# Moving one product per head pair to GpSimd and its mask to ScalarE, with reordered VectorE steps

## The chip, the cores and the metric

The kernel runs on one core of a Trainium2 chip. The metric is the device time of one execution in microseconds (us): 1022.77 us before the change, the median of three runs from 1022.21 to 1023.84. All profile times are of one profiled execution whose span is 1027.5 us.

The engines are named as the profile names them: PE is TensorE (matmuls and transposes), DVE is VectorE, ACT is ScalarE, POOL is GpSimd, SP issues the DMAs.

## The reference

For 8 batches and 8 heads, with 576 rows of 64 numbers each:

```
scores = (q @ k.T) / sqrt(64)                 # 576 x 576 per head
kth    = the 32nd largest score of each row
scores = where(scores >= kth, scores, -1e9)
attn   = softmax(scores);  out = attn @ v
```

The heads of a row are then joined to 512 numbers, and 4608 such rows go through a mixture of experts: a gate picks one of 8 experts per row, each expert keeps the 80 rows with the largest gate weight, and for these two matmuls with a relu between them are computed. All other rows of the output are zero. This change touches the attention part alone.

## The kernel before

**Pairs and units.** Two heads are handled together as a pair; there are 32 pairs. The 576 query rows of a pair are cut into four blocks of 128 rows and one of 64. A unit is one head's block (128 rows by 576 scores). The 64-row blocks of both heads lie in one unit, since together they fill 128 partitions. So a pair has 9 units: places 0 to 7 are head 0 and head 1 of block 0, 1, 2, 3, and place 8 is the joint last unit. There are 288 units in all (NU). "Odd" units are those whose work is shifted away from DVE; before the change these are places 1, 3, 5 and 7.

**What a unit needs.** `front` computes scores on PE into a PSUM tile of four banks, of which there is only one (`four`, tag `sp`), and ACT copies them to the SBUF tile `s` (L206). DVE finds the 24 largest scores of each row: six maxima of 96 columns (`parts`, L213), then three maxima and two replacements over these 48 candidates (`search`, L224 and L232). ACT then writes `sign`, the sign of (24th largest minus score), and counts it (L229). The product `y` = s times sign (L236) makes another maximum over the whole row (L238, `w<-y`) give the largest scores below the 24th. The small operation `pick` (L241) selects the threshold by the count. The `mask` of scores below the threshold is made by POOL for even units (L254, a compare) and by ACT for odd ones (L250, a relu). `turn_w` transposes the scores on PE (L286) and adds the mask by further matmuls on top (L291); ACT takes the exponentials (L293, L295) into `wT`; `back` multiplies by v on PE (L309); `divide` scales the result on ACT (L330).

**The pipeline.** The order of all instructions is written out by hand in `run`. Each call of `step(i)` starts one unit and carries older ones on: unit i has its six maxima taken, unit i-1 its search, unit i-2 its product, unit i-3 its large maximum, unit i-4 its pick and mask. A string of letters gives the order of the DVE work in a step: G is one maximum of 96 columns; a, b, c, d, e are the five stages of the search (after e, ACT's sign is issued); y is the product; g the maximum over y; h the pick; m the mask; z the reciprocals (L321). After the letters, the step issues `turn_w` for unit i-4 when a block is complete, `divide`, `front` for unit i+4, `back` for unit i-5, the transposes of the next pair's q and k (`turn`), and one piece of `norm`, which for a finished pair transposes the output (copied by L342), multiplies it by the gate weights (L347) and copies these few columns out on ACT (L353, `part`). Each engine executes its instructions in exactly this order. A step below is named by its place: the step of place p handles the maxima of place p and the mask of place p-4 (counted round the pair).

So in the step of place 3, the order is: mask of place 8; sign of place 2; then on PE `turn_w` of place 8 (transposes, then the mask matmuls), `back` of place 7, and L347; on ACT the exponentials of place 8 and the copy of `part`. In the step of place 4 follow, on PE, `front` and `back` of place 8, and in the step of place 5 `turn_w` of places 0 and 1.

**Which engine the product runs on.** For odd units POOL, for the others DVE:

```
engine = nc.gpsimd if i in self.odd else nc.vector
engine.tensor_tensor(out=y, in0=s, in1=sign, op=Alu.mult)
```

There is one `y` buffer, two of `sign`, three of `mask` and two of `wT`. POOL gets, in program order, the mask of unit i-4 ahead of the product of unit i-2.

## Time and profile before

| engine | busy us | share of the span | instructions |
|---|---|---|---|
| PE (matmul) | 902.3 | 88% | 13381 |
| DVE | 896.0 | 87% | 5087 |
| ACT | 786.2 | 77% | 1671 |
| POOL | 456.1 | 44% | 331 |

The attention part takes the first 890 us or so; the rest is routing and the experts. The busy share alone does not say who sets the pace, because an instruction that is held up after it has started counts as busy. The groups of instructions concerned:

| line, engine, what | count | mean ns |
|---|---|---|
| L236 DVE product | 160 | 739 |
| L236 POOL product | 128 | 1281 |
| L254 POOL mask | 159 | 1721 |
| L250 ACT mask | 128 | 777 |
| L241 DVE pick | 288 | 290 |
| L189 ACT copies of qT, kT | 32 + 32 | 642, 647 |

### The profile page before, as it was taken

Reading aid. Unit: us, or ns where it says so; the run is one execution under the profiler, and the core shown is the slowest. Engines: PE = TensorE matmul, PEld = TensorE weight load, DVE = VectorE, ACT = ScalarE, POOL = GpSimd, SP = SyncE. Lnnn points to the kernel's source line nnn. Section 1 sums busy time; section 2 is a strip of 40 time slices with the busy share of each in tenths; the row PEclk is TensorE's granted clock in tenths of the full one; section 3 lists DMA queues with packets and bytes.
Section 4 is the critical chain, followed back from the end, with each engine's and each line's share of the span. In section 5 each row is a group of like instructions: output and inputs, shape, how many; then the busy total and the mean of one; then the engine's idle time right before and its main releaser. Section 6 shows DMA issues by size and latency. Waiting matters only on the chain.

```text
span 1027.5 us, 35579 instructions
## 1 busy us (share of the span) xinstructions
PE 902.3 (88%) x13381; PEld 728.9 (71%) x13381; DVE 896.0 (87%) x5087; ACT 786.2 (77%) x1671; POOL 456.1 (44%) x331
## 2 busy tenths in 40 slices
PE   5889999999889999989899999998999998598896
PEld 3677777777667777777677777776777777588886
DVE  3999999999999999999999999999999999551000
ACT  3888899888888898888898888898888988401110
POOL 1444555554454545554454544555454554211101
PEclk9999999999999999999999999999999999879998
DMA  4344443333333323233333311111221200326800
GB/s 93 77 118 129 122 128 89 89 89 89 90 88 89 80 72 81 77 81 84 85 89 89 89 41 38 46 45 48 48 49 48 49 13 14 119 77 214 325 23 25
DMA packets 167893, 85.76 MB, mean 83 GB/s; under 512 B 117792, under 2 KB 154656, under 8 KB 167712
## 3 DMA queue, kind: packets, MB, share of 16 engines
q1 hardware_dynamic: 166688, 80.78, 28.4%
q0 software_dynamic: 1024, 2.62, 0.8%
q8 instruction: 107, 1.75, 0.7%
q14 instruction: 74, 0.61, 0.2%
HBM read 63.19 MB, written 20.19 MB: 81 GB/s over the span
## 4 chain that ended last, share of the span: by engine, by line
DVE 54%; PE 30%; ACT 11%; issue 2%; another core or an unknown queue 1%; DMA 0%; SPq 0%; POOL 0%; POOLq 0%; ACTq 0%; DVEq 0%
DVE cand L213 17%; DVE w L238 12%; PE cc L309 7%; DVE cand L232 6%; DVE y L236 6%; DVE pick L241 4%; DVE top L224 4%; PE yp L776 3%; PE sp L201 3%; PE ab L286 3%; ACT wT L295 3%; PE sp L178 2%; ACT sign L229 2%; PE warm L632 2%; DVE w L224 2%
## 5 line engine op out<-in xcount | busy, mean ns | idle before, releaser
L213 DVE MAX8 cand<-s 128x8 f32<-128x96 f32 x1728 | 387.0, 244 | 9.5 <-ACT s L206 9.5
L254 POOL TENSOR_SCALAR mask<-s,thr_all 128x576 bf16<-128x576 f32 x159 | 273.7, 1721 | 199.6 <-PE ab L291 130.6
L309 PEld LDWEIGHTS cc<-vb,wT 128*64 128x64 f32 x5760 | 201.2, 139 | 111.5 <-ACT wT L295 94.6
L236 POOL TENSOR_TENSOR y<-s,sign 128x576 f32<-128x576 f32 x128 | 164.0, 1281 | 240.3 <-ACT sign L229 104.2
L309 PE MATMUL cc<-vb,wT 128*64 128x65 f32 x5760 | 223.4, 225 | 52.1 <-ACT wT L295 52.1
L229 ACT ACTIVATE sign<-s,w 128x576 bf16<-128x576 f32 x288 | 226.0, 785 | 44.9 <-DVE w L224 44.5
L238 DVE MAX8 w<-y 128x8 f32<-128x576 f32 x288 | 217.4, 755 | 2.2 <-POOL y L236 2.0
L201 PE MATMUL sp<-kT,qT 64*128 64x288 f32 (+1 forms) x1280 | 202.0, 435 | 14.7 <-ACT part L353 6.1
L286 PE MATMUL ab<-ident,s 128*128 128x128 f32 x1152 | 176.5, 282 | 10.9 <-ACT wT L295 10.9
L206 ACT ACTIVATE s<-sp 128x1152 f32<-128x1152 f32 (+1 forms) x160 | 167.2, 1045 | 11.4 <-PE sp L201 9.8
L286 PEld LDWEIGHTS ab<-ident,s 128*128 128x128 f32 x1152 | 128.3, 142 | 34.6 <-ACT wT L295 25.1
L295 ACT ACTIVATE wT<-ab 128x1024 f32<-128x1024 f32 (+1 forms) x160 | 150.8, 942 | 0.0
L201 PEld LDWEIGHTS sp<-kT,qT 64*128 64x128 f32 (+1 forms) x1280 | 105.5, 179 | 53.4 <-ACT part L353 8.0
L236 DVE TENSOR_TENSOR y<-s,sign 128x576 f32<-128x576 f32 x160 | 118.2, 739 | 3.1 <-ACT sign L229 2.6
L224 DVE MAX8 top<-cand 128x8 f32<-128x48 f32 x576 | 114.4, 199 | 0.1
L291 PEld LDWEIGHTS <-mask 128*128 128x128 bf16 x1440 | 94.5, 98 | 25.8 <-ACT mask L250 19.0
L232 DVE MATCH_REPLACE8 cand<-top,cand 128x48 f32<-128x48 f32 x576 | 110.0, 191 | 0.0
L250 ACT ACTIVATE mask<-s,thr_all 128x576 bf16<-128x576 f32 x128 | 99.5, 777 | 0.4 <-DVE pick L241 0.4
L330 ACT ACTIVATE xn<-cc,z_all 128x64 f32<-128x64 f32 (+1 forms) x320 | 82.8, 316 | 2.3 <-DVE z_all L321 2.3
L241 DVE SCALAR_TENSOR_TENSOR pick<-past,cnt,w 128x9 f32<-128x9 f32 x288 | 83.6, 290 | 0.0
L286 PE MATMUL cc<-ident,s 128*128 128x128 f32 x288 | 79.0, 274 | 0.2 <-ACT xn L330 0.2
L293 ACT ACTIVATE wT<-cc 128x256 f32<-128x256 f32 (+1 forms) x160 | 57.5, 359 | 6.0 <-PE cc L291 4.4
(192 smaller groups left out, 981.5 us busy)
## 6 DMA issues: line engine op xcount, KB each, us to landing
w<-in_moe_w_dram SPq DMA_DIRECT2D x32, 512.0 KB, 4.3
w<-in_moe_w_dram SPq DMA_DIRECT2D x8, 2048.0 KB, 12.6
out_dram<-zero SPq DMA_DIRECT2D x9, 1024.0 KB, 5.9
qn<-in_q_dram SPq DMA_DIRECT2D x64, 128.0 KB, 2.4
kn<-in_k_dram SPq DMA_DIRECT2D x64, 128.0 KB, 2.5
vb<-in_v_dram SPq DMA_DIRECT2D x64, 128.0 KB, 2.5
xd<-xn SPq DMA_DIRECT2D x32, 256.0 KB, 4.1
qn<-in_q_dram SPq DMA_DIRECT2D x32, 32.0 KB, 2.3
```

The lines of the kernel that those rows point to most:

```text
L201: nc.tensor.matmul(o, lhsT=qT[d, t * P : t * P + m], rhs=kT[d, j * HS : (j + 1) * HS], start=True, stop=True)
L206: nc.scalar.activation(s[:, : g * S].rearrange("p (j c) -> p j c", c=HS), ps[:, : 2 * g, :HS], Act.Copy, scale=TINY)
L213: nc.vector.max(out=cand[:, j, :], in_=s[:, j * S // NG : (j + 1) * S // NG])
L224: nc.vector.max(out=dst, in_=cand)
L229: nc.scalar.activation(sign, s, Act.Sign, bias=w9[:, 7:8], scale=-1.0, accum_out=cnt)
L232: nc.vector.match_replace(out=cand, in_to_replace=dst, in_values=cand, imm_value=LOW)
L236: engine.tensor_tensor(out=y, in0=s, in1=sign, op=Alu.mult)
L238: nc.vector.max(out=w9[:, 8:], in_=y)
L254: engine.tensor_scalar(self.mask[i], self.s[i], self.thr[:, i : i + 1], None, op0=Alu.is_lt)
L286: nc.tensor.matmul(dst[h][c], lhsT=sc[:, keys[c]], rhs=ident, start=c == 0 or (c == NF and h == 0), stop=False, is_transpose=True, skip_gr ...
L295: nc.scalar.activation(wT[:, : g * NF, :], ab.rearrange("p h c r -> p (h c) r")[:, : g * NF, :], Act.Exp, scale=scale / TINY)
L309: nc.tensor.matmul(cc[r : r + TL, o], lhsT=wT[:, j * NF + c if c < NF else 2 * NF + j, r0 : r0 + TL], rhs=vb[:, c, h, :], start=(c == 0), ...
```

## The change

Place 8 of each pair becomes odd too. Its product moves from DVE to POOL, and its mask from POOL (DVE for the very last unit) to ACT, where the matmul with `huge` replaces that with `minus`. The order of the letters is rewritten: where unit i-3 is odd, so that its product was made by POOL in the step before, two maxima and one replacement (G, b, G) are put ahead of the pick; otherwise the large maximum g goes first and the pick after it. The sign (after e) comes early where unit i-1 is odd. The copies of the transposed q and k out of PSUM become one operation.

```
-            self.turned[n] = [self.qkp.tile([P, S], F32, name=name, tag=name) for name in ("qT", "kT")]
-            for j in range(2):
-                nc.scalar.copy(self.turned[n][j], ps[j][:, :S])
+            both = self.qkp.tile([P, 2, S], F32, name="both", tag="both")
+            nc.scalar.copy(both, four.rearrange("p (k j) c -> p k (j c)", k=2)[:, :, :S])
+            self.turned[n] = both[:, 0, :], both[:, 1, :]
...
-            engine = nc.vector if i == NU - 1 else nc.gpsimd
-            engine.tensor_scalar(self.mask[i], self.s[i], self.thr[:, i : i + 1], None, op0=Alu.is_lt)
+            nc.gpsimd.tensor_scalar(self.mask[i], self.s[i], self.thr[:, i : i + 1], None, op0=Alu.is_lt)
...
-            self.odd = {i for i, unit in enumerate(units) if unit[2] == 1}
+            self.odd = {i for i, unit in enumerate(units) if unit[2] > 0}
...
-                for c in "hmgyGbGcGdGGGeaz" if i - 2 in self.odd else "hmgGbGcGdGeGGyaz":
+                head = "GbGhmg" if i - 3 in self.odd else "ghmGbG"
+                rest = "GeGGa" if i - 1 in self.odd else "GGGea"
+                for c in head + ("ycGd" + rest if i - 2 in self.odd else "cGd" + rest[:-1] + "ya") + "z":
```

What it is for: DVE has one product less per pair, and the pick, a DVE operation with two tensor inputs, comes later in the steps that follow a POOL product.

## The prediction

> **What bounds the kernel now.** I read the windows first, then the groups, then the timelines of four engines over one pair. In the window from 300 to 400 us (columns: window, its length, busy PE, weight loads, DVE, ACT, POOL, then granted clock, DMA share and GB/s):

> ```profile
> 300.00:400.00 100.00, 90.69 (x1277) 72.32 (x1277) 100.00 (x583) 89.77 (x190) 50.26 (x34) 1.00 0.34 90
> ```

> DVE is busy 100.00 of 100 us, so it sets the pace. But PE and ACT stand at 90%, and each waits for the other inside; whether they have room must be seen in their order. A group of instructions (count, busy us and mean ns, idle time before them), and one line of the waits (total us, times, longest):

> ```profile
> L236 DVE TENSOR_TENSOR y<-s,sign 128x576 f32<-128x576 f32 x160 | 118.2, 739 | 3.1 <-ACT sign L229 2.6
> ```

> ```profile
> ACT sign L229 <- DVE w L224: 44.5, 67, 1.5
> ```

> ACT waits for DVE only 44.5 us in 32 pairs, 1.4 us per pair, two waits of about 0.6. Now the timelines. POOL and DVE at the end of one pair's heavy part:

> ```profile
> 345.19 1.72 POOL L254 TENSOR_SCALAR mask<-s,thr_all 128x576 bf16<-128x576 f32 x1 [4.61 <-PE ab L291]
> 346.88 1.28 POOL L236 TENSOR_TENSOR y<-s,sign 128x576 f32<-128x576 f32 x1
> ```

> ```profile
> 347.25 0.93 DVE L241 SCALAR_TENSOR_TENSOR pick<-past,cnt,w 128x9 f32<-128x9 f32 x1
> ```

> A pick normally takes 0.21; this one ends at 348.18, just as POOL's product ends at 348.16. It was held by that product, 0.8 us in every pair, and is counted as busy. ACT, then PE, in the steps of places 2 to 5:

> ```profile
> 347.72 1.16 ACT L206 ACTIVATE s<-sp 128x1152 f32<-128x1152 f32 x1
> 348.73 0.81 ACT L229 ACTIVATE sign<-s,w 128x576 bf16<-128x576 f32 x1
> ...
> 350.45 0.19 ACT L353 COPY part<-sp 128x40 f32<-128x40 f32 x1 [0.16 <-PE sp L347]
> ...
> 353.87 0.78 ACT L229 ACTIVATE sign<-s,w 128x576 bf16<-128x576 f32 x1 [0.63 <-DVE w L224]
> 354.55 0.19 ACT L229 ACTIVATION_READ_ACCUMULATOR sign<-s,w 128x1 f32 x1
> 354.80 0.38 ACT L293 ACTIVATE wT<-cc 128x256 f32<-128x256 f32 x1
> ```

> ```profile
> 348.11 0.22 PE L291 MATMUL cc<-minus,mask 128*128 128x128 bf16 x1
> 348.16 0.39 PE L291 MATMUL ab<-minus,mask 128*128 128x128 bf16 x4
> 348.48 1.39 PE L309 MATMUL cc<-vb,wT 128*64 128x65 f32 x40
> 349.69 0.71 PE L347 MATMUL sp<-wg,xT 128*64 128x8 f32 x20
> 350.69 1.19 PE L201 MATMUL sp<-kT,qT 64*64 64x288 f32 x8 [0.29 <-ACT part L353]
> 351.81 1.38 PE L309 MATMUL cc<-vb,wT 128*64 128x65 f32 x20
> 353.12 0.66 PE L286 MATMUL ab<-ident,s 128*128 128x128 f32 x4
> ...
> 354.55 0.22 PE L291 MATMUL cc<-huge,mask 128*128 128x128 bf16 x1
> ```

> PE runs without a gap, but for `part`, from place 8's mask matmuls (348.11) to those of places 0 and 1, after which ACT's exponential can start (354.80). The sign at 348.73 comes about 1.5 us after its input was ready: ACT is behind here, which costs nothing as long as POOL made the mask in time.

> [...] a DVE product ran from 878.91 to 879.67 in its usual 0.76 us while a mask ran from 877.95 to 879.67, so a mask holds nothing after its first 0.96 us. [...]

> **Part by part.** A step of DVE from start to start in the timeline: pick 0.13, g 0.67, six G 0.98, b and d 0.17 each, c, e 0.11 each, a 0.12: 2.46 us; 3.12 with a product (0.66). Nine steps before: 9 x 2.46 + 5 x 0.66 + reciprocals and the gate addition 0.45 + the held pick 0.80 = 26.7; the trace has 26.73 from one pair to the next.

> *Product of place 8 to POOL.* Takes 0.66 off DVE per pair. But in the step of place 1 POOL now has the mask of place 6 and then the product of place 8. Before, the same double stood in the step of place 3 (mask of 8, product of 1). From a pick the chain is 0.39 + 1.72 + 1.28 = 3.37 us, and the next pick comes 2.47 later, in the old order and in the new (both picks move by the same G, b, G, 0.5 us). So the hold of 0.8 stays, moved from the step of place 4 to that of place 2. POOL's sum falls (32 products of 1.28 for 31 masks of 1.72).

> *Later picks.* They keep picks clear of late products in the steps of places 4, 6, 8: worth the 0.1 seen at place 8 in some pairs. Pick to DVE product shrinks from 2.34 to 1.84 us, while POOL's mask ends 2.11 after the pick. If masks excluded products to their end, three products per pair would lose 0.27 each; I take zero, by the 878.91 line, and keep 0.8 for the range. DVE alone would then need 26.73 - 0.66 = 26.07 per pair.

> *One copy for two.* Starts of the two are 0.54 + 0.53 apart; one of 1152 columns takes 1.01 like the score copy (347.72 to 348.73). Saves 0.06 of ACT.

> *Mask of place 8 to ACT.* It goes in ahead of the sign at 348.73 and adds 0.68 (start of a mask to start of a following sign). ACT gets there at 348.73 - 0.06 = 348.67, whatever DVE does, for ACT has no wait on DVE from the sign at 332.78 on. Queued behind it: on ACT the sign of place 2; on PE, which now waits for it, everything from 348.11 on. A mask takes 0.79 and PE starts 0.05 later, so at 349.51 instead of 348.11. Then mask matmuls 0.37, `back` 1.21, L347 up to the copy 0.76: `part` at 351.85 instead of 350.45, **1.40 later**.

> That closes a loop of ACT and PE. Before: exponential 328.08 to the sign of place 6, without its wait 4.03; that sign (332.78) to the sign of place 2 (348.73) 15.95, all ACT or PE work that ACT waits for (the q and k transposes 1 us among it); to `part` 1.72; to the next such exponential 4.35. Sum 26.05: 0.68 shorter than DVE's 26.73, which is why it isn't seen. After: 26.05 + 1.40 = **27.45**. The old slack takes 0.68 of the 1.40 and 0.72 per pair is lost. DVE, with 26.07 of work, will then stand waiting.

> *Sum.* 31 rounds x 0.72 = 22.3. Three rounds before are longer on DVE by the gate work, 1.85 each (27.84 + 27.47 against 2 x 26.73); about half of that will hide in DVE's idle time: -2.8. At the end, mask and product of the last unit on slower engines: DVE's mask was 0.52, ACT's is 0.78 behind exponentials, +0.7. Together +20.2: **1043 us**.

> **The rivals.** *Faster, DVE's law:* ACT and PE follow after all and each pair gains 0.66: 32 x 0.66 - 0.7 = 20.4, so 1002. For it speaks the 100% of DVE; against it the 1.40 above, over twice the slack. *No change:* the mask costs ACT 0.62 but PE does not pass the delay on to `part`; then the product of place 2 still waits for its sign. Its slack is 0.75 now (350.40 against 349.64), and DVE comes 0.66 earlier, ACT 0.62 later, so it loses 0.55 or so and 0.1 per pair is left: 1021. *Masks exclude products:* DVE at 26.07 + 0.81 = 26.88, 31 x 0.15 = 5: 1028, if the loop is not there. *The loop at full weight:* nothing of the 1.40 absorbed, 31 x 1.40 = 43: 1066. *The hold goes away as well:* 32 x 1.46: 976; it needs POOL's 3.37 to fit in 2.47.

> **How the numbers follow.** Forecast 0.65, DVE's law 0.15, no change 0.12, masks exclude 0.03, full weight 0.03, hold gone 0.02. The range leaves out DVE's law, the hold and the full weight (0.20): from 1018, below the no-change case, to 1050, if gate work hides nothing and a lowered PE clock lengthens the loop. Slower: 0.65 + 0.03 + 0.03 and 0.03 of the no-change case = 0.74; same 0.05; faster 0.21.

> **What would show it.** PE's wait ahead of L291 for ACT's mask grows from 12.7 us to over 40; ACT waits ahead of `part` about 1 us per pair (4.5 us in all before) and ahead of the exponential of place 1 about 0.8; ACT's wait for DVE's `w` nearly vanishes; DVE is no longer at 100%, with waits before L236 for ACT's sign; pairs are 27.4 us apart. A held pick of about 0.9 us stands in the step of place 2. It would be wrong if ACT reached place 8's mask early, or if PE made up the 1.4 us before `part`.

## The result and the profile after

The changed kernel takes 1069.68 us (median, 1063.06 to 1073.34) against 1022.49 us for the kernel before: a ratio of 1.0455, with a 95% interval from 1.0392 to 1.0517. It is slower, as forecast, but by 47 us where 20 were forecast, and it lies outside the range that ended at 1050. Its runs are spread over 10 us; those of the kernel before over 3.

The windows of the kernel after (window, its length, then busy PE, weight loads, DVE, ACT, POOL, granted clock, DMA share, GB/s), and the row of the page with the granted PE clock in 40 slices:

```profile
100.00:200.00 100.00, 88.17 (x1160) 68.93 (x1159) 90.88 (x526) 83.42 (x176) 44.27 (x31) 0.93 0.37 96
300.00:400.00 100.00, 87.16 (x1228) 68.58 (x1226) 95.74 (x553) 88.07 (x183) 47.02 (x32) 1.00 0.29 75
```

```profile
PEclk9999989889899999998899999989999999988999
```

In the window from 300 to 400 us DVE has fallen from 100.00 to 95.74: it no longer sets the pace. In the window from 100 to 200 there is something else: the clock is 0.93 and DVE is busy only 90.88. Slices with an 8 in the clock's row are scattered over the whole attention part.

Pairs are therefore of two kinds. Measured from one pair to the next at the same operation of DVE (the last maximum of the search, L224, for place 6), the period is 27.62 us where the clock is full, 26.73 before; and about 2.9 us more in 8 of 31 pairs. The waits of the kernel after (us in total, times, longest), and the first of them in the kernel before:

```profile
PE cc L289 <- ACT mask L250: 53.1, 65, 1.3
DVE z_all L319 <- PE cc L307: 30.7, 39, 4.8
ACT part L351 <- PE sp L345: 29.2, 23, 2.3
ACT wT L291 <- PE cc L289: 28.9, 32, 2.0
DVE lg L354 <- ACT part L351: 17.6, 22, 2.6
ACT sign L229 <- DVE w L224: 8.6, 15, 0.8
```

```profile
PE cc L291 <- ACT mask L250: 12.7, 30, 0.4
```

(Lines after L188 have moved: the mask matmuls are L289, `back` is L307, the gate weights' matmul L345, `part` L351, the exponentials L291 and L293.) PE's wait for ACT's mask has gone from 12.7 to 53.1 us, ACT waits for PE twice per pair, and ACT's wait for DVE has shrunk from 44.5 to 8.6. One pair at full clock, PE first, around place 8's mask matmuls:

```profile
650.99 0.66 PE L284 MATMUL ab<-ident,s 128*128 128x128 f32 x4 [0.32 <-ACT wT L293]
653.09 0.23 PE L289 MATMUL cc<-huge,mask 128*128 128x128 bf16 x1 [1.33 <-ACT mask L250]
...
653.47 1.39 PE L307 MATMUL cc<-vb,wT 128*64 128x65 f32 x40
655.68 1.19 PE L201 MATMUL sp<-both 64*64 64x288 f32 x8 [0.29 <-ACT lg L351]
```

Then ACT in the same steps:

```profile
652.23 0.80 ACT L250 ACTIVATE mask<-s,thr_all 128x576 bf16<-128x576 f32 x1
652.89 0.80 ACT L229 ACTIVATE sign<-s,w 128x576 bf16<-128x576 f32 x1
...
655.44 0.19 ACT L351 COPY lg<-sp 128x40 f32<-128x40 f32 x1 [1.00 <-PE sp L345]
...
659.79 0.38 ACT L291 ACTIVATE wT<-cc 128x256 f32<-128x256 f32 x1 [0.75 <-PE cc L289]
...
664.02 0.78 ACT L229 ACTIVATE sign<-s,w 128x576 bf16<-128x576 f32 x1
```

And DVE:

```profile
653.82 0.76 DVE L236 TENSOR_TENSOR y<-s,sign 128x576 f32<-128x576 f32 x1 [0.30 <-ACT sign L229]
654.90 0.17 DVE L319 RECIPROCAL z_all<-cc 128x2 f32<-128x2 f32 x1 [0.21 <-PE cc L307]
658.29 0.16 DVE L319 RECIPROCAL z_all<-cc 64x2 f32<-64x2 f32 x1 [0.74 <-ACT mask L250]
663.72 0.20 DVE L224 MAX8 w<-cand 128x8 f32<-128x48 f32 x1
672.80 0.92 DVE L241 SCALAR_TENSOR_TENSOR pick<-past,cnt,w 128x9 f32<-128x9 f32 x1
```

The loop of the forecast stands here: PE waits 1.33 us for the mask that ACT reaches at 652.23, the copy of the gate result follows late, ACT waits for it (1.00) and again for PE at the exponential (0.75). The held pick (672.80, 0.92) now stands in the step of place 2. DVE waits too: for the sign, and twice for the reciprocals of `back`'s sums. The 0.74 ahead of the second is put down to ACT's mask, but that had ended at its usual time; the reciprocal reads what `back` of place 8 writes, a matmul group that started at 656.80 and took 1.38, and it starts as that ends.

The slow pairs look different. Here is PE at the same place in one of them:

```profile
134.90 0.23 PE L289 MATMUL cc<-huge,mask 128*128 128x128 bf16 x1 [1.33 <-ACT mask L250]
...
135.28 2.09 PE L307 MATMUL cc<-vb,wT 128*64 128x65 f32 x40
137.15 1.19 PE L345 MATMUL sp<-wg,xT 128*64 128x8 f32 x20
138.63 2.19 PE L201 MATMUL sp<-both 64*64 64x288 f32 x8 [0.28 <-ACT part L351]
140.74 2.20 PE L307 MATMUL cc<-vb,wT 128*64 128x65 f32 x20
```

The wait is the same 1.33 us, but right after it `back` takes 2.09 us instead of 1.39, the scores of place 8 take 2.19 instead of 1.19, and the next `back` 2.20 instead of 1.38. The trace also records each change of the granted clock. In this execution it has only two values, 1 and 0.5, and all its changes lie on one grid of 3.41 us. These are windows of that grid, four around this wait and two around the wait (up to 341.7) of a pair at full clock:

```profile
132.31:135.73 3.42, 1.78 (x26) 1.28 (x26) 3.14 (x21) 3.42 (x9) 2.33 (x2) 1.00 0.09 19
135.73:139.14 3.41, 3.12 (x55) 2.81 (x52) 1.48 (x5) 1.28 (x4) 0.00 (x0) 0.50 0.03 7
139.14:142.55 3.41, 3.41 (x25) 2.28 (x22) 2.15 (x16) 2.24 (x7) 1.27 (x1) 0.50 0.00 0
142.55:145.97 3.42, 3.42 (x36) 2.69 (x35) 2.99 (x17) 1.84 (x6) 1.72 (x1) 1.00 0.58 148
...
337.12:340.53 3.41, 2.54 (x21) 1.52 (x18) 3.41 (x24) 3.41 (x8) 1.28 (x1) 1.00 0.50 112
340.53:343.95 3.42, 2.28 (x65) 2.11 (x65) 2.90 (x15) 2.49 (x6) 1.72 (x1) 1.00 0.02 5
```

The clock is half for two windows, 6.83 us, and it falls at the end of a window in which PE was busy 1.78 us. In the other pair the same weak stretch of PE is split between two windows, with 2.54 and 2.28 us busy, and the clock stays full. The place on the grid separates all pairs: in the 8 slow ones the wait ends 2.57 to 2.75 us into a window, in the 23 others 0.63 to 2.44 us into one. (Busy time as the profile shows it does not separate them: five windows with 1.77 or 1.78 us busy, whose waits end at 2.40 to 2.44, brought no drop.) Slow pairs without gate work take 30.54 us: 30.54 - 27.62 = 2.9 us for a stretch.

So the profiled run (1072.98 us, near the top of the spread) divides like this, measured from place 6 of the first pair to place 6 of the last: 883.3 us against 835.6, 47.7 more; the 8 slow pairs, about 2.9 us each, are 23.4 of them, the clock's part, and 24.3 are the longer loop.

### The profile page after: what moved, and what is told of

It reads as the page before. It is cut to its first block, busy times and chain, and to the rows that moved or that the text cites. A ratio compares the mean times of both kernels' runs of the same rounds, so it can differ in the third digit from the quotient of the medians.

```text
span 1070.8 us, 35577 instructions
## 1 busy us (share of the span) xinstructions
PE 924.3 (86%) x13381; PEld 740.3 (69%) x13381; DVE 886.4 (83%) x5054; ACT 800.7 (75%) x1671; POOL 443.6 (41%) x332
## 4 chain that ended last, share of the span: by engine, by line
PE 38%; ACT 32%; DVE 25%; issue 4%; POOL 0%; DMA 0%; SPq 0%; ACTq 0%; POOLq 0%; DVEq 0%
PE cc L307 13%; DVE cand L213 8%; ACT wT L293 7%; ACT sign L229 6%; ACT s L206 6%; ACT mask L250 6%; DVE w L238 5%; PE sp L201 5%; PE sp L178 4%; PE yp L776 4%; DVE cand L232 3%; DVE y L236 3%; ACT wT L291 2%; PE ab L284 2%; ACT xn L328 2%
## 5 line engine op out<-in xcount | busy, mean ns | idle before, releaser
L213 DVE MAX8 cand<-s 128x8 f32<-128x96 f32 x1728 | 392.4, 248 | 10.1 <-ACT s L206 9.5
L236 POOL TENSOR_TENSOR y<-s,sign 128x576 f32<-128x576 f32 x160 | 205.0, 1281 | 361.4 <-ACT sign L229 128.5
L307 PEld LDWEIGHTS cc<-vb,wT 128*64 128x64 f32 x5760 | 211.0, 143 | 98.7 <-ACT wT L293 78.4
L252 POOL TENSOR_SCALAR mask<-s,thr_all 128x576 bf16<-128x576 f32 x128 | 220.3, 1721 | 139.6 <-DVE pick L241 130.8
L307 PE MATMUL cc<-vb,wT 128*64 128x65 f32 x5760 | 233.5, 230 | 35.8 <-ACT wT L293 35.8
L229 ACT ACTIVATE sign<-s,w 128x576 bf16<-128x576 f32 x288 | 225.0, 781 | 11.2 <-DVE w L224 8.6
L201 PE MATMUL sp<-both 64*128 64x288 f32 (+1 forms) x1280 | 210.0, 449 | 14.5 <-ACT part L351 6.1
L206 ACT ACTIVATE s<-sp 128x1152 f32<-128x1152 f32 (+1 forms) x160 | 167.0, 1044 | 23.0 <-PE sp L201 23.0
L293 ACT ACTIVATE wT<-ab 128x1024 f32<-128x1024 f32 (+1 forms) x160 | 150.2, 939 | 0.0
L201 PEld LDWEIGHTS sp<-both 64*128 64x128 f32 (+1 forms) x1280 | 107.8, 183 | 55.4 <-ACT part L351 8.0
L289 PEld LDWEIGHTS <-mask 128*128 128x128 bf16 x1440 | 91.5, 98 | 71.3 <-ACT mask L250 65.7
L250 ACT ACTIVATE mask<-s,thr_all 128x576 bf16<-128x576 f32 x160 | 124.9, 780 | 1.2 <-DVE pick L241 1.0
L224 DVE MAX8 top<-cand 128x8 f32<-128x48 f32 x576 | 115.9, 201 | 1.1
L236 DVE TENSOR_TENSOR y<-s,sign 128x576 f32<-128x576 f32 x128 | 95.5, 746 | 10.2 <-ACT sign L229 10.0
L241 DVE SCALAR_TENSOR_TENSOR pick<-past,cnt,w 128x9 f32<-128x9 f32 x288 | 83.5, 290 | 0.0
L289 PE MATMUL cc<-huge,mask 128*128 128x128 bf16 x160 | 36.4, 227 | 53.1 <-ACT mask L250 53.1
```

The lines of the kernel that those rows point to most:

```text
L201: nc.tensor.matmul(o, lhsT=qT[d, t * P : t * P + m], rhs=kT[d, j * HS : (j + 1) * HS], start=True, stop=True)
L206: nc.scalar.activation(s[:, : g * S].rearrange("p (j c) -> p j c", c=HS), ps[:, : 2 * g, :HS], Act.Copy, scale=TINY)
L213: nc.vector.max(out=cand[:, j, :], in_=s[:, j * S // NG : (j + 1) * S // NG])
L229: nc.scalar.activation(sign, s, Act.Sign, bias=w9[:, 7:8], scale=-1.0, accum_out=cnt)
L250: nc.scalar.activation(self.mask[i], self.s[i], Act.Relu, bias=self.thr[:, i : i + 1], scale=-1.0)
L252: nc.gpsimd.tensor_scalar(self.mask[i], self.s[i], self.thr[:, i : i + 1], None, op0=Alu.is_lt)
```

## The experiments

The theory after the result was: the loop of ACT and PE is as long as forecast and gives half of the loss; the idle 1.3 us on PE brings half-clock stretches, which give the other half. The rivals: the mask on ACT costs in another way (ACT's own time, or a branch through DVE); the product or the new order are to blame; the slow clock has nothing to do with the idle stretch. All ratios are to the kernel before, run on the same chip.

**The mask of place 8 alone on ACT** (kernel before, product on DVE, old order; the mask matmul takes `huge` with it; `self.last` holds the units of place 8):

```
-            if i in self.odd:
+            if i in self.odd or i in self.last:
                 nc.scalar.activation(self.mask[i], ...)
```

> The kernel before with one edit: the mask of place 8 goes to ACT (product of place 8 stays on DVE, old order of the letters, two copies). Theory (the mask, late in ACT's queue, holds PE up and closes the loop of ACT and PE, and the gap on PE lets its clock drop): pairs 27.6 us apart where the clock is full, stretches at half clock as in the changed kernel, 1050 to 1075 us. Rival (the product on POOL or the new order of the letters costs the time; DVE alone sets the pace): the pick of the step of place 4 is no longer held, since POOL has no mask ahead of the product of place 1, so 26.73 - 0.80 per pair and about 998 us.

Measured: 1090.51 us, 1.0600 (1.0544 to 1.0657). The mask alone brings the loss, and a larger one than the whole change; the time also lies above the 1075 expected at most. A pair at full clock takes 28.2 us (27.62 in the whole change), and 5 pairs have half-clock stretches, again just those whose wait ends in one part of the grid (2.55 to 2.88 us into a window). The trace shows waits that go with the extra 0.6; DVE, then ACT of this kernel:

```profile
606.27 0.20 DVE L356 TENSOR_TENSOR lg<-lg,part 128x40 f32<-128x40 f32 x1 [0.59 <-ACT part L353]
```

```profile
592.52 0.78 ACT L229 ACTIVATE sign<-s,w 128x576 bf16<-128x576 f32 x1 [0.45 <-DVE w L224]
```

In the pairs that have a gate addition, three of four, the late `part` holds up this addition on DVE, DVE is then late with `w`, and ACT's sign waits for it. In the others, DVE waits 0.74 us for the sums of a late `back` instead. A branch of the loop runs through DVE; the forecast had none.

**The product of place 8 alone on POOL** (kernel before, mask on POOL, old order; the letter y stands where that order has it for POOL's products):

```
-            engine = nc.gpsimd if i in self.odd else nc.vector
+            engine = nc.gpsimd if i in self.odd or i in self.last else nc.vector
```

> The kernel before with one edit: the product of place 8 goes to POOL (mask of place 8 stays on POOL, old order, two copies). Theory: no effect on the loop of ACT and PE; DVE loses 0.66 of work per pair and gains a second held pick of about 0.8 in the step of place 2, so 26.9 per pair and 1022 to 1030 us, clock as before. Rival (the product on POOL is what costs): 1045 us or more.

Measured: 1032.32 us, 1.0037 (1.0022 to 1.0051); 26.88 us per pair. DVE's 0.66 is taken off, but POOL now runs late in two steps and two picks per pair are held (0.92 and 0.91) where it was one: + 0.70. That makes 26.77; the last 0.1 was not traced. The forecast's argument that a mask followed by a product on POOL makes a held pick stands, here twice.

**PE kept busy while it waits** (kernel after, 12 matmuls on zeros into a part of `ab` that this unit does not use, between the transposes and the mask matmuls of place 8):

```
+            if g == 1:
+                for _ in range(12):
+                    nc.tensor.matmul(<256 columns of ab, bank 1>, lhsT=zeros, rhs=zeros, start=True, stop=True)
             for h in range(g):
                 mk = self.mask.pop(i + h)
```

> The changed kernel with twelve idle matmuls of 256 columns on PE between the transposes and the mask matmuls of place 8, whose result is never read: they fill the 1.3 us in which PE waits for ACT's mask. Theory (the gap makes the PE clock drop, and the drops are what the forecast of 1043 lacked): mean clock 0.985 or more, pairs 27.6 apart throughout, 1040 to 1047 us. Rival (the clock drops for another reason, such as the amount of PE work, or the loss lies elsewhere): clock 0.965 to 0.975 still and 1063 to 1075 us.

Measured: 1054.99 us, 1.0277 (1.0250 to 1.0304), with a clock of 0.991 over the run (after: 0.965). PE of this kernel:

```profile
661.69 1.47 PE L289 MATMUL ab<-zero 128*128 128x256 bf16 x12
663.18 0.23 PE L293 MATMUL cc<-huge,mask 128*128 128x128 bf16 x1
```

More work on PE made the kernel faster (the time lies above the 1040 to 1047 expected, but the kernel before took 1028.36 on this chip). Apart from the first and the last few, every pair without gate work takes 27.62 us: the loop is untouched, and no half-clock stretch is left in the attention part of its trace. That shows the cause of the second half of the loss. Up to place 6 of the last pair it takes 24.1 us more than the kernel before, which is the loop, and 23.4 less than the change as it is.

**`back` of place 7 ahead of `turn_w` of place 8** (kernel after; PE has 1.2 us of work to do before it needs the mask):

```
+                joint = whole(i - 4) and units[i - 4][2] == 2
+                if joint:
+                    self.back(*units[i - 5][:2])
                 if whole(i - 4):
                     self.turn_w(*units[i - 4][:2])
```

> The changed kernel with one edit in the order of PE: in the step of place 3, back of place 7 is issued ahead of turn_w of place 8, so that PE multiplies by v while ACT makes the mask. Theory (PE's wait for the mask delays everything behind it up to the exponential of place 1): part comes about 1.2 us earlier, the loop falls to 26.4, no gap on PE in this step; pairs 26.4 apart, 1003 to 1015 us, clock 0.98 or more. Rival (ACT itself is full with one mask more, whatever PE does): 27.4 per pair and 1040 us or more.

Measured: 1024.82 us, 0.9966 (0.9953 to 0.9978); 26.63 us per pair, clock 0.984. Two calls changed places and the whole loss is gone (a ratio of 0.9966 after 1.0455): PE's order was what turned the late mask into a longer loop. The 26.4 expected was not reached, and a wait on DVE fits that (26 such waits, 10.6 us in all):

```profile
615.82 0.76 DVE L236 TENSOR_TENSOR y<-s,sign 128x576 f32<-128x576 f32 x1 [0.31 <-ACT sign L229]
```

This is the forecast's rival "no change", worked out there as 0.1 per pair won: the product of place 2 waits for its sign, which stands behind the mask in ACT's queue. Measured 26.73 - 26.63 = 0.1. That this wait alone sets the pace was not isolated.

**The mask still later** (kernel after, mask of place 8 issued behind the sign of place 2 on ACT):

```
+                if i - 4 in self.last:
+                    head, rest = "ghGbG", "GGGema"
```

> The changed kernel with the mask of place 8 moved further back in ACT's queue, behind the sign of place 2 instead of ahead of it (m after e in the step of place 3). No work is added. Theory: PE waits for the mask 0.75 us longer than 1.33, all behind it moves by that, pairs 28.2 to 28.4 apart where the clock is full, more half-clock stretches, 1085 to 1110 us. Rival (ACT's amount of work sets the pace, not the place of the mask): no change, 1063 to 1075.

Measured: 1133.45 us, 1.1074 (1.1056 to 1.1093), with a clock of 0.925. PE, then a line of the waits, then the row of the clock:

```profile
329.22 0.23 PE L289 MATMUL cc<-huge,mask 128*128 128x128 bf16 x1 [2.08 <-ACT mask L250]
```

```profile
PE cc L289 <- ACT mask L250: 76.6, 65, 2.3
```

```profile
PEclk9999898988998899989898898989998989988999
```

The wait of PE is 0.75 longer, as meant, and the loop grows by as much. Only three pairs have no half-clock stretch. They follow gate work and take 28.95 to 28.96 us; pairs at the same places take 28.20 in the change. So a plain pair at full clock would take 27.62 + 0.76 = 28.4, as expected. All 28 others have a stretch: 12 of 3.41 us, with periods of about 29.9 in plain pairs, and 16 of 6.83 us, with about 31.3. The time is above the 1110 expected at most because the longer wait brings the clock down in 28 of 31 pairs, where 1.33 us did in 8.

**The new order alone** (kernel before with the new letters, product and mask where they were):

```
-                for c in "hmgyGbGcGdGGGeaz" if i - 2 in self.odd else "hmgGbGcGdGeGGyaz":
+                head = "GbGhmg" if i - 3 in self.odd else "ghmGbG"
+                rest = "GeGGa" if i - 1 in self.odd else "GGGea"
+                for c in head + ("ycGd" + rest if i - 2 in self.odd else "cGd" + rest[:-1] + "ya") + "z":
```

> The kernel before with the new order of the letters alone (odd units, masks and copies as before). Theory: DVE still sets the pace, with the same work and about the same held pick in the step of place 4 (0.8 to 1.0 us): 26.7 to 26.95 per pair, 1020 to 1028 us. Rival (later picks delay masks and so PE): 1035 us or more.

Measured: 1027.96 us, 1.0049 (1.0032 to 1.0066); 26.95 per pair. Alone it wins nothing: the held pick takes 1.09 instead of 0.93 and stays in the step of place 4, because pick and POOL's product move together.

**The mask of place 8 on DVE** (kernel after; product on POOL, order new; the mask matmul takes `minus` with it):

```
+            engine = nc.vector if i in self.last else nc.gpsimd
+            engine.tensor_scalar(self.mask[i], self.s[i], self.thr[:, i : i + 1], None, op0=Alu.is_lt)
```

> The changed kernel with the mask of place 8 made by DVE, right after the pick, instead of ACT. The loop of ACT and PE then has its old length of 26.0; DVE has 25.3 of work, a mask of about 0.55 with its wait for the pick, and the held pick of 0.7 in the step of place 2: 26.5 per pair, no gap on PE, clock 0.98 or more, 1012 to 1020 us. Rival (the product on POOL or ACT's load costs, not the place of the mask): 1040 or more.

Measured: 1027.02 us, 1.0043 (1.0026 to 1.0060); 26.77 per pair, clock 0.986. With the mask off ACT, the longer loop and the slow pairs behind PE's wait are both gone. The 1012 to 1020 expected was missed. DVE is full again (busy 99.75 of the 100 us from 300 to 400), and its bill closes: its 26.07 of the forecast plus about 0.65 for a mask of 0.52 and the gap ahead of it is 26.72.

**The same, with POOL's product of place 8 ahead of its mask of place 6:**

```
+                if i - 2 in self.last:
+                    head = "ghyGbGm"     # and no y later in this step
```

> As the one before, and in the step of place 1 POOL makes the product of place 8 ahead of the mask of place 6. This takes the product away from the pick of place 7, which falls 0.9 us into that mask instead. If a mask holds no pick after its first part: no held pick, DVE at 25.8, the loop of ACT and PE at 26.0 sets the pace, 998 to 1006 us. If a mask holds a pick to its end: 0.8 is held, 26.6 per pair, 1014 to 1020.

Measured: 1002.50 us, 0.9799 (0.9783 to 0.9815); 26.12 per pair. This beats both kernels. POOL, DVE and the window of this kernel:

```profile
331.92 1.28 POOL L236 TENSOR_TENSOR y<-s,sign 128x576 f32<-128x576 f32 x1 [1.10 <-DVE pick L241]
333.17 1.72 POOL L253 TENSOR_SCALAR mask<-s,thr_all 128x576 bf16<-128x576 f32 x1
```

```profile
334.00 0.21 DVE L241 SCALAR_TENSOR_TENSOR pick<-past,cnt,w 128x9 f32<-128x9 f32 x1
```

```profile
300.00:400.00 100.00, 92.53 (x1314) 73.59 (x1312) 99.50 (x593) 91.11 (x192) 51.24 (x35) 1.00 0.31 79
```

No pick is held any more: the one at 334.00 takes 0.21 in the middle of POOL's mask (333.17 to 334.89). In this trace 31 picks begin 0.55 to 0.83 us into a mask, and none takes more than 0.22. In the kernel after, the pick at 672.80 began 0.40 us into POOL's product (672.40 to 673.68) and took 0.92, to the end of it; here the picks that begin 0.55 us or more into a mask are not held. No pick of this trace falls in the first half microsecond of a mask. DVE is at 99.50 of 100 us again; the loop of ACT and PE, 26.05 by the forecast, is about as long, and which of the two sets the pace was not separated.

**12 matmuls on zeros in the kernel before** (same place as above; the mask stays on POOL):

```
+            if g == 1:
+                for _ in range(12):
+                    nc.tensor.matmul(<256 columns of ab, bank 1>, lhsT=zeros, rhs=zeros, start=True, stop=True)
```

> The kernel before, with 12 matmuls of 256 columns on zeros put on PE between the transposes and the mask matmuls of place 8: PE work of about 1.3 us (661.7 to 663.0 in the filled kernel after), of no use to the result, and the mask stays on POOL. If the loop of ACT and PE is what the mask of place 8 lengthened, then any 1.3 us at this spot does the same: 26.05 + 1.3 = 27.35 per pair in place of 26.73, 31 x 0.62 = 19 us more, and as PE is never idle there no half-clock stretch: 1042 us, from 1036 to 1046. If it is the mask on ACT itself (ACT's time, or DVE waiting for the mask) that made the loop longer, the fill only uses PE time that was free: 1023, within 4.

Measured: 1059.25 us, 1.0359 (1.0345 to 1.0373); 28.0 us per pair, clock 0.989. The loss needs no mask on ACT: any 1.3 us on PE at this spot gives it. But the pair grew by all of the 1.3 us, where the loop of ACT and PE has 0.68 of slack. DVE and ACT show what took the slack:

```profile
648.89 0.16 DVE L325 RECIPROCAL z_all<-cc 64x2 f32<-64x2 f32 x1 [0.73 <-ACT mask L250]
...
654.63 0.61 DVE L241 SCALAR_TENSOR_TENSOR pick<-past,cnt,w 128x9 f32<-128x9 f32 x1
```

```profile
660.76 0.78 ACT L229 ACTIVATE sign<-s,w 128x576 bf16<-128x576 f32 x1 [0.41 <-DVE w L224]
```

DVE is full in the kernel before. In this pair it stands 0.73 us for the sums of a `back` that is late and 0.40 for a second held pick: 26.73 + 0.73 + 0.40 = 27.9. (In the pairs with a gate addition it stands 0.59 us for `part` instead.) In this order the branch from PE through DVE to ACT's sign has no slack at all.

**6 of the 12 matmuls in the kernel after:**

```
-                for _ in range(12):
+                for _ in range(6):
```

> The kernel after with 6 of the 12 idle matmuls: 0.65 us of the 1.33 us that PE waits for ACT's mask is filled, 0.7 us stays idle. Pairs at full clock should stay at 27.62, since the fill ends before the mask does. If PE's being idle in this one place is what brings the half-clock stretches, and the activity has a threshold, half the fill may already be enough: clock .99, ratio to before about 1.028 as with 12. If every idle stretch counts in proportion, about half of the clock loss stays: some 4 slow pairs of 31, ratio about 1.037. If the fill of 12 worked otherwise (a coincidence of the chip), the ratio is 1.045.

Measured: 1053.43 us, 1.0295 (1.0281 to 1.0309), clock 0.987. PE of this kernel:

```profile
661.60 0.82 PE L289 MATMUL ab<-zero 128*128 128x256 bf16 x6
663.09 0.23 PE L293 MATMUL cc<-huge,mask 128*128 128x128 bf16 x1 [0.68 <-ACT mask L250]
```

An idle stretch of 0.68 us in every pair brings no slow pair; one of 1.33 brought 8 in 31. Five of the shorter waits end 2.61 to 2.93 us into a window of this run's grid, where the long ones brought slow pairs, so this is not luck with the grid. The effect sets in between these two lengths, and it is not in proportion to the idle time.

**One copy of q and k alone** (kernel before):

```
-            for j in range(2):
-                nc.scalar.copy(self.turned[n][j], ps[j][:, :S])
+            nc.scalar.copy(both, four.rearrange("p (k j) c -> p k (j c)", k=2)[:, :, :S])
```

> The kernel before with the merged copy of q and k alone. By my account it saves 0.06 us of ACT per pair, where ACT has slack in the kernel before: no change, 1022.5 within 2 us. The rival: the one copy gives the PSUM tile back later or earlier to the next front, and PE's order in the step moves; then the pair's period moves by more than 0.05 and the time by more than 2 us.

Measured: 1022.29 us, 0.9991 (0.9985 to 0.9998); 26.75 per pair. The medians differ by 0.7 us; the merged copy explains nothing of the loss.

**Product and mask moved, old order** (kernel before with one edit):

```
-            self.odd = {i for i, unit in enumerate(units) if unit[2] == 1}
+            self.odd = {i for i, unit in enumerate(units) if unit[2] > 0}
```

> The change without its new letter order and without the merged copy: the product of place 8 on POOL and its mask on ACT, in the old order of the DVE work. The mask alone gave 28.2 us per pair, the whole change 27.62; this tells which of product and order makes the difference. If it is the product (0.66 less work on DVE, which was the branch through the reciprocals, the pick and the sign), the pair at full clock is 27.6, within 0.15, and the ratio is 1.04 to 1.055 with the clock stretches. If it is the order (the pick kept off the late products and the gate addition), the pair stays at 28.1 to 28.3 and the ratio is near 1.06. In both cases PE is idle 1.3 us ahead of place 8's mask matmuls and some pairs have half-clock stretches.

Measured: 1088.39 us, 1.0565 (1.0528 to 1.0603); 28.25 per pair at full clock, with 7 slow pairs (their waits end 2.52 to 2.98 us into a window of the grid, no other does). It is the order, then, and not the product, that makes the change shorter by 0.6 per pair than the mask alone. Taking 0.66 us off DVE bought nothing while DVE stood waiting for PE. In the waits of this kernel:

```profile
ACT sign L229 <- DVE w L224: 21.3, 38, 1.5
```

This is 8.6 with the new order: (21.3 - 8.6) / 32 = 0.4 per pair, for `w` comes earlier. That the rest is the second held pick (most take about 0.64 in the step of place 8, where the new order has 0.21) is read from the trace and was not isolated.

## Why the forecast was wrong

**Right: the direction and its mechanism.** Every sign that was named appeared: PE's wait for ACT's mask over 40 us (53.1), ACT's two waits of about 1.0 and 0.8 (1.00 and 0.75), ACT's wait for DVE nearly gone (8.6), waits ahead of DVE's product, DVE below 100%, the held pick of 0.92 in the step of place 2. The experiments with the mask alone, with the mask on DVE and with `back` first show that the late mask, passed on by PE's order, is the cause.

**Nearly right: the period.** Forecast 27.45, measured 27.62 at full clock. The parts: from `part` to the exponential 4.35 as before (655.44 to 659.79); from the sign of place 2 to `part` 2.55 where 2.50 follows from the forecast; from the exponential to the sign of place 6 it is 4.23 (659.79 to 664.02) instead of 4.03. This 0.20 is a short wait for `w`, which DVE finished only at 663.92, late by its waits for PE. The forecast let DVE "stand waiting" and took that as free; DVE's waits feed back into ACT's sign. The fill in the kernel before and the run with the old order show how large this branch can become: 28.0 and 28.25.

**Wrong: the sum.** The step that failed is the sum "Together +20.2": it has no term for the PE clock. A lowered clock stands only among the reasons for the range, up to 1050. In the profiled run the clock takes 23.4 us, as much as the loop, which takes 24.3 where 22.3 - 2.8 = 19.5 was forecast. By the times alone the clock's part is less: 1.0455 against 1.0277 and 1.0295 with PE kept busy is 16 to 18 us of 1022. The profiled runs also differ from 148.9 to 158.2 us behind that last place 6, which follows none of the edits and whose cause was not sought.

The sign was there to read. The forecast had PE wait 1.4 us in every pair, and asked only who would wait for PE. The profile of the kernel before has PE at half clock twice in its attention part, behind waits of 1.91 and 2.28 us for ACT's exponentials, which end at 496.62 and 868.55. Windows of its grid, each time the one with the wait and the one behind it:

```profile
493.21:496.62 3.41, 1.51 (x13) 0.85 (x11) 3.34 (x24) 2.10 (x5) 2.25 (x2) 1.00 0.22 80
496.62:500.03 3.41, 3.40 (x44) 2.96 (x44) 3.41 (x21) 2.13 (x5) 1.08 (x2) 0.50 0.00 0
...
865.26:868.67 3.41, 1.08 (x17) 0.72 (x15) 3.41 (x26) 2.73 (x7) 2.71 (x2) 1.00 0.26 77
868.67:872.08 3.41, 3.41 (x46) 3.29 (x47) 3.41 (x21) 1.76 (x5) 1.28 (x1) 0.50 0.06 14
```

Two other waits of 1.91 us there (they end at 280.59 and 712.98) brought no drop. In the kernel after 1.33 us was enough, in a window with PE busy 1.78 us, 52% of it, and of these equal waits only those bring a drop that end 2.57 us or more into a window. As the pairs are not tied to this grid (their waits end 0.63 to 2.75 us into a window), the number of drops may vary from run to run; that is an estimate, for only one execution of each kernel was traced. It would fit the spread of 10 us: the four runs of the kernel after have mean clocks of 0.963, 0.965, 0.971 and 0.976, and their times fall in this order from 1073.34 to 1063.06.

**Wrong, small: the gate work.** Half of three times 1.85 us was to hide in DVE's idle time. In the filled kernel, at full clock, the two rounds still take 28.7 and 28.2, 1.1 and 0.6 above their neighbours: 1.7 instead of 1.85. About 0.5 us hides, not 2.8.

**The rivals.** "No change" came true once `back` went first. "DVE's law" needed the mask off ACT; with POOL's order changed as well, that kernel takes 1002.5 us. "Masks exclude" is refuted by the changed kernel itself: 72 of its DVE products begin inside a POOL mask (1.07 us into it or later), and none takes more than 0.76 us; the pick at 334.00 says the same. "The loop at full weight" (1066) is near the measured time, but by coincidence: the slack was absorbed in the change, and the clock filled the gap.

## What to carry to other kernels

When a change makes PE wait in a place where it did not wait before, cost two things: who waits for PE, through every engine and also the one believed idle, and whether its clock falls behind the wait, as it did here at the end of windows of 3.41 us in which PE was busy 1.78 us or less. A wait of 1.3 us per pair cost as much through the clock as through the loop in the profiled run, and 16 to 18 of 47 us by the times. If the wait can't be avoided, look for work that is already there to put ahead of it: here `back` removed both costs (26.63 us per pair and a clock of 0.984, where the kernel before has 26.73 and 0.983).
